# A second matrix product in two halves of the array that exchange their banks

## The chip, the cores and the metric

The kernel runs on one core of one Trainium2 chip. What is compared is the time on the device in microseconds of one execution. The engines are PE (TensorE, matrix products), DVE (VectorE), ACT (ScalarE), POOL (GpSimd) and SP (SyncE, which here issues transfers and waits).

## What is computed

A short convolution over the tokens of each of 8 sequences (7 taps, one softmax-normalised set of taps for each of 8 groups of 24 channels), and then a feed-forward part on each of the 31232 tokens:

```python
# B, S, D = 8, 3904, 192; H, K = 8, 7; d_ff = 1024
w = softmax(weight, axis=-1)                     # (H, K)
y[b, s, h, :] = sum_k w[h, k] * x_pad[b, s + k, h, :]     # 6 rows of zeros ahead of each sequence
a = y @ w1                                       # (31232, 1024)
b = y @ w2
h = a * b @ w3                                   # elementwise a*b, then (1024, 1024)
out = h @ w_out                                  # (31232, 192), float32
```

## The kernel before

Since nothing stands between the last two products, the kernel forms `W = w3 @ w_out` (1024 x 192, `W_sb`, eight tiles of 128 rows) once on the chip. For each token there are then two stages, here called the first and the second product: `a * b` (bf16, `abT`, 128 feature rows at a time, tokens along the free side), and `abT` times `W_sb`.

**Rounds.** The tokens lie in two streams of 15616 (`r` = 0 and 1, `NS = 2`). A round `R` takes 512 tokens of each stream (`CH`); there are 31 rounds, the last of 256. `abT` of a round is `[128, 8, 2, 512]`.

**First product** (`first_product`, L618 to L651). The depth is 192, cut into three pieces of 64 (`NP`, `Q`). Stream 0 has its channels on partitions 0 to 63 and stream 1 on 64 to 127, so matmuls use 64 rows of the array (64*128 in the profile) and come in pairs, one on each half, with 512 columns, into the two banks of a PSUM tile. For each of 8 feature tiles there are three pairs for `a` (`pa`) and three for `b` (`pb`). ACT casts `pa` to bf16 (`asb`, L640), DVE multiplies it with `pb` into `abT` (L643).

**Second product** (`second_product`, L653 to L677). For one round and stream: four groups of 128 tokens, eight feature tiles each, 32 matmuls with 128 rows and 192 columns (128*128 in the profile, L659), where the tile of `abT` is the loaded weight and `W_sb` streams. Two groups share a bank: group `g` lies in bank `g // 2`. ACT copies the two banks to `osb` (L664), SP stores `osb` (L673).

**PSUM.** All PSUM tiles are of one kind, `[128, 2, 512]` float32, two banks each (`banks`, L104). There are four, given out in turn.

**Phases.** The loop at L901 runs over 11 phases. In most of them it does the first product of three rounds (`rounds`) and then the second product of the same three rounds (`ends`), both streams of each. Phases are numbered `p` = 0 to 10 here, as in the code. In phases 0, 2 and 5 (`places`) part of the convolution is done on PE between the second products (`convolve`).

**The convolution of the other tokens.** For the phases in `SIDE` the convolution is a sum of scaled shifts, done on DVE (`side_sums`, six steps of about 1.3 us for a task, placed among the second products by `side_steps`) and on POOL (`pool_sums`). ACT does a first step of each (`side_first`, `pool_first`). Their inputs are brought in and transposed by DMA: `side_transpose` (L515) and `pool_transpose` (L568). Tokens convolved on PE are stored to DRAM and come back through `transposes` (L449, three or two transposes for a round).

**Order.** The schedule is by hand (`manual_schedule`): each engine's queue holds its instructions in the order in which the program issues them. All transposes and all result stores are on SP's queue. In the loop, after the first products of a phase: `turn(p)` issues the `transposes` that are due and whose place in the ring of rounds is free; then come the `pool_transpose` and `side_transpose` of the phase; then, for each round and stream, the second product with its copy and store and the side steps; at the end the `late` ones of `side_transpose` and another `turn(p)`.

Of the kernel before, what the change touches and what calls it, by code (L numbers as in the profile page):

```python
# [16 lines left out]
def kernel(  # L17
# [10 lines left out]
    nc = tc.nc  # L28

    B, S, D = x.shape  # L30
# [3 lines left out]
    JT = DFF // 128  # L34
    PAD = K - 1

    NS = 2
    TS = B * S // NS
    CH = 512
# [4 lines left out]
    Q = 64  # L44
# [59 lines left out]
    def banks(name):  # L104
        return psum.tile([128, NS, CH], FP32, tag="banks", name=name)
# [4 lines left out]
    def slot(shape, dtype, name):  # L110
        return stage.tile(shape, dtype, tag="slot", bufs=6, name=name)

    rows = dram.tile([TS, NP * NS * Q], BF16, name="rows")
# [15 lines left out]
    def group(r, e):  # L129
        return slice((2 * r + e) * C, (2 * r + e) * C + C)  # L130
# [57 lines left out]
    for r in range(NS):  # L188
        p = group(r, 0).start
# [110 lines left out]
    p = group(1, 0).start  # L300
# [3 lines left out]
    for k in range(2):  # L304
# [3 lines left out]
            start=(k == 0), stop=(k == 1))  # L308
# [134 lines left out]
    def transposes(R, first=0):  # L443
        t0, t1 = max(R * CH, first), min((R + 1) * CH, TS)
        a = ring_of[R] * CH % RING + t0 - R * CH
        for k in range(NP):
            if beside(phase_of(R), k):
                continue
            nc.sync.dma_start_transpose(  # L449
                out=xT[k][:, a:a + t1 - t0], in_=rows[t0:t1, k * 128:(k + 1) * 128])  # L450
# [98 lines left out]
    def pool_tiles():  # L549
        for t in (stage.tile([128, 3 * CH + HALO], BF16, tag="wo", bufs=1, name="acc"), pool_more):  # L550
            pool_acc.append(t[:, 0:2 * CH].bitcast(FP32))
            pool_raw.append(t[:, 2 * CH:3 * CH + HALO])

    def part_tile():
        t = work.tile([128, XN], BF16, tag="xb", bufs=5, name="side")
        o = 0
        for q, ks in PART.items():
            n = len(ks) * 2 * CH
            side_of[q] = t[:, o:o + n].rearrange("p (k t) -> p k t", k=len(ks))
            o += n  # L560
# [5 lines left out]
    def pool_transpose(lane, p, k, half):  # L566
        _, _, t0, _ = pool_half(p, k, half)
        nc.sync.dma_start_transpose(out=pool_raw[lane], in_=rows_c[t0 - HALO:t0 + CH, k, :])  # L568

    def pool_first(lane, p, k, half):  # L570
        nc.scalar.activation(
            out=pool_acc[lane], in_=pool_raw[lane][:, HALO - 1:HALO - 1 + CH],
            func=ACT.Copy, scale=wC[:, k, K - 2:K - 1])
# [39 lines left out]
    abT_of, asb_of = {}, {}  # L613

    def width(R):
        return min(CH, TS - R * CH)
# [33 lines left out]
            if between and f0 in between:  # L650
                between[f0]()  # L651

    def second_product(R, r, later=None):  # L653
        ab = abT_of[R]
        ng = width(R) // 128
        ops = banks("ops")
        for g in range(ng):
            for jt in range(JT):
                nc.tensor.matmul(  # L659
                    ops[:, g // 2, (g % 2) * D:(g % 2) * D + D],  # L660
                    ab[:, jt, r, g * 128:(g + 1) * 128], W_sb[:, jt, :],
                    start=(jt == 0), stop=(jt == JT - 1))
        osb = slot([128, ng, D], FP32, "osb")
        nc.scalar.copy(out=osb.rearrange("p (a g) d -> p a (g d)", g=2),  # L664
                       in_=ops[:, 0:ng // 2, 0:2 * D])
        n = ng if R < NR - 4 else ng // 2
        for g in range(0, ng, n):
            t0 = r * TS + R * CH + g * 128
            send = (nc.scalar if g and (R, r) == (NR - 1, NS - 2) else nc.sync).dma_start
            args = dict(out=out[t0:t0 + n * 128, :].rearrange("(g p) d -> p g d", p=128),  # L670
                        in_=osb[:, g:g + n, :])
            if later is None:
                send(**args)  # L673
            else:
                later.append(lambda send=send, args=args: send(**args))
        if r == 1:
            del abT_of[R]  # L677
# [15 lines left out]
    W_sb = const.tile([128, JT, D], BF16)  # L693
# [69 lines left out]
    phases = [((), trios[0])] + [(t, t) for t in trios[1:-1]] + \  # L763
        [(trios[-1], trios[-1][:1]), ((NR - 1,), trios[-1][1:] + (NR - 1,))]

    def stage_of(R):
        return R // TRIO

    places = {0: (1, 2, 3, 4), 2: (0, 1, 2, 3), 5: (0, 1, 3)}
# [4 lines left out]
    starts, chain, begun, room, p = {}, {}, set(), 0, -1  # L774
    for i, cost, f in steps:
        while room < cost:
            p += 1
            room = rooms[p]
            at, ends = 0, {}
            starts.setdefault(p, [])  # L780
        if i not in begun:
            begun.add(i)
            starts[p].append(i)
            n = max(p == 0, int(at) // 2 - 1, -(-ends.get(i - 2, 0) // 2))
# [9 lines left out]
    def side_steps(p, n, state):  # L794
        items = chain.get(p, [])
        for v, (i, at, f) in enumerate(items):
            if at is not None and at <= n and v not in state:
                state.add(v)
                f()
        for v, (i, at, f) in enumerate(items):  # L800
            if at is None and v not in state:
                state.add(v)
                f()
            elif v not in state:
                break
# [46 lines left out]
    for p, b, part, n in ((1, 5, 0, 0), (1, 5, 1, 4), (3, 6, 0, 0), (4, 6, 1, 0)):  # L852
        todo = x_jobs(b, part)
        n = n or len(todo)
        jobs[p] += todo[:n]
        jobs[p + 1] += todo[n:]
    pool_from = {p - 1: v for p, v in POOL_AT.items()}
# [11 lines left out]
    sent, rest, results = [LAG + 3], [], []  # L869
# [20 lines left out]
    def turn(p):  # L890
        while due and stage_of(due[0]) <= p + 2 and \
                stage_of(conv_rounds[ring_of[due[0]] - RING // CH]) <= p:
            transposes(due.pop(0))

    def clear():
        for b in list(zero_rows):
            for xb, p0, w in zero_rows.pop(b):
                nc.gpsimd.memset(xb[p0:p0 + PAD, w, :], 0.0)

    pace = const.tile([1, 2], BF16)  # L900
    for p, (rounds, ends) in enumerate(phases):  # L901
        todo = jobs.pop(p, [])

        last = len(points) - 1
        lanes = pool_sum.pop(p, ())
        counts = [0] * 7 if len(lanes) > 1 else [0] * 3 + [2] * 4 if p == 1 else [2] * 2 + [1] * 5
        at = [[todo.pop(0) for _ in range(min(n, len(todo)))] for n in counts + [len(todo)]]
        if p in places:
            at[last - 1].insert(0, clear)
        elif len(lanes) > 1:  # L910
            at[last].insert(0, clear)
        for fs in lanes:
            for v, f in enumerate(fs):
                at[v if len(lanes) == 1 else 0].append(f)
        if p == 3:
            part_tile()

        def issue(R, ft, fs):
            def run():
                P(out=pace, in_=abT_of[R][0:1, ft, 1, 0:2] if ft else asb_of[0][0:1, 1, 0:2])  # L920
                for f in fs:
                    f()
            return run

        for j, R in enumerate(rounds):
            first_product(R, {ft: issue(R, ft, at[v])
                              for v, (a, ft) in enumerate(((0, 0),) + points[1:] if
                                                          len(lanes) > 1 else points)
                              if a == j and at[v]})
        assert not todo  # L930
        if len(lanes) < 2:
            clear()
        if p == 0:
            pool_tiles()
        turn(p)
        raws = starts.get(p + 1, ())
        late = [i for i in raws if p == 0 or len(lanes) > 1 or i >= 5 and chain[p][0][0] <= i - 5]
        if p > 1:
            for lane, t in enumerate(pool_from.get(p, ())):
                pool_transpose(lane, *t)  # L940
        for i in raws:
            if i not in late:
                side_transpose(i)
        if p == 1:
            pool_transpose(0, *pool_from[p][0])
        state = set()
        side_steps(p, 0, state)
        for n, (R, r) in enumerate((R, r) for R in ends for r in range(NS)):
            if (R, r) == (NR - 1, NS - 1):
                last_product(R, r)  # L950
            else:
                second_product(R, r, results if p == 0 else None)
            if n == 4 and len(pool_from.get(p, ())) > 1:
                for lane, t in enumerate(pool_from[p]):
                    pool_first(lane, *t)
            if n in places.get(p, ()):
                convolve(p)
            side_steps(p, n + 1, state)
        assert len(state) == len(chain.get(p, ()))
        while results:  # L960
            results.pop(0)()
        for b, js in rest:
            store(b, js=js)
        rest.clear()
        for i in late:
            side_transpose(i)
        turn(p)
# [31 lines left out]
```

## Time and profile before

| | us |
|---|---|
| median of 3 runs | 510.65 (510.35 to 510.77) |
| the profiled execution | 510.84 |
| its span | 509.1 |

| engine | busy us | share | instructions |
|---|---|---|---|
| PE matmuls | 504.4 | 99% | 5732 |
| PE weight loads (PEld) | 335.9 | 66% | 5732 |
| DVE | 446.2 | 88% | 402 |
| ACT | 349.6 | 69% | 390 |
| POOL | 255.9 | 50% | 340 |

All stretches of the span show PE's granted clock at nine tenths or more of full speed. In the rows of the time line the columns are the start in us, the time in us from the first start to the last end of the merged instructions, engine, line, operation, what is written and read, and the number of instructions; a bracket holds idle time before them and what ended it. SPq is the queue of SP. In the rows of the chain of waits the columns are start, duration, engine, tile and line. In the rows of a stretch (`197.30:213.30`) they are its length, the busy time of PE, PEld, DVE, ACT and POOL with the number of instructions, the granted clock of PE, and the share and rate of the DMA engines.

### The profile page before, as it was taken

What the parts mean: (1) busy time and instruction counts of PE and PEld (TensorE: products, weight loads), DVE (VectorE), ACT (ScalarE), POOL (GpSimd) and SP (SyncE); (2) the same over time, 40 slices, a digit from 0 to 9 for tenths busy, and PEclk for the clock granted to TensorE, in tenths of its full rate; (3) what the DMA queues carried; (4) which work ended last, traced back from release to release, by engine and by line L of the source; (5) the groups of instructions that cost most, each with busy time, mean ns of one, the idle gap of its engine ahead of it and who ended that gap; (6) DMA issues with size and microseconds to landing.
All of it is one profiled execution on the core that took longest, in us unless ns stands there. A gap on an engine that the chain in (4) does not pass through costs nothing.

```text
span 509.1 us, 13680 instructions
## 1 busy us (share of the span) xinstructions
PE 504.4 (99%) x5732; PEld 335.9 (66%) x5732; DVE 446.2 (88%) x402; ACT 349.6 (69%) x390; POOL 255.9 (50%) x340
## 2 busy tenths in 40 slices
PE   8999999999999999999999999999999999999997
PEld 4546864595569557845874596569457855965697
DVE  7898769999999799999999998999999999999930
ACT  6786667746779776577567878763876577457752
POOL 9975201332890799499879945992371056000000
PEclk9999999999999999999999999999999999999999
DMA  9999978999969769980998097629302400230025
GB/s 136 160 170 162 166 150 182 149 156 182 175 41 181 136 150 108 227 110 13 100 232 103 12 167 145 117 29 202 83 1 76 155 2 1 93 96 1 1 65 156
DMA packets 161113, 58.46 MB, mean 115 GB/s; under 512 B 116895, under 2 KB 161051, under 8 KB 161051
## 3 DMA queue, kind: packets, MB, share of 16 engines
q1 hardware_dynamic: 86107, 40.12, 37.7%
q0 software_dynamic: 74784, 17.37, 37.3%
q8 instruction: 45, 0.74, 0.6%
q14 instruction: 17, 0.14, 0.1%
q10 hardware_dynamic: 160, 0.10, 0.1%
HBM read 35.02 MB, written 34.85 MB: 137 GB/s over the span
## 4 chain that ended last, share of the span: by engine, by line
PE 99%; ACT 0%; DVE 0%; issue 0%
PE ops L659 32%; PE pa L633 31%; PE pb L633 31%; PE cps L345 1%; PE wps L731 1%; PE warm L246 1%; PE tps L420 0%; PE ops L684 0%; DVE abT L643 0%; PE tps L435 0%; PE cps L375 0%; ACT asb L640 0%; ACT convo L355 0%; PE bps L305 0%; PE warm L258 0%
## 5 line engine op out<-in xcount | busy, mean ns | idle before, releaser
L643 DVE TENSOR_TENSOR abT<-asb,pb 128x1024 bf16<-128x1024 bf16 x240 | 292.7, 1221 | 29.4 <-ACT asb L640 13.4
L640 ACT CAST asb<-pa 128x1024 bf16<-128x1024 f32 x244 | 247.0, 1012 | 64.0 <-PE pa L633 63.8
L633 PEld LDWEIGHTS <-wn 64*128 64x128 bf16 x1488 | 138.5, 94 | 82.1 <-issue 1.6
L633 PEld LDWEIGHTS <-ws 64*128 64x128 bf16 x1488 | 130.1, 94 | 70.8 <-issue 0.9
L659 PE MATMUL ops<-W_sb,abT 128*128 128x192 bf16 x1936 | 163.5, 246 | 0.0
L659 PEld LDWEIGHTS <-abT 128*128 128x128 bf16 x1936 | 158.6, 98 | 6.3 <-issue 6.3
L664 ACT COPY osb<-ops 128x768 f32<-128x768 f32 (+1 forms) x61 | 48.5, 796 | 81.8 <-PE ops L659 80.0
L633 PE MATMUL pb<-xT,wn 64*128 64x512 bf16 x376 | 103.7, 376 | 0.0
L633 PE MATMUL pa<-xT,ws 64*128 64x512 bf16 x376 | 103.5, 376 | 0.0
L633 PE MATMUL pa<-xT,wn 64*128 64x512 bf16 x376 | 103.0, 376 | 0.1
L633 PE MATMUL pb<-xT,ws 64*128 64x512 bf16 x376 | 102.2, 376 | 0.0
L633 PE MATMUL pb<-side,wn 64*128 64x512 bf16 (+1 forms) x368 | 100.4, 369 | 0.0
L633 PE MATMUL pa<-side,ws 64*128 64x512 bf16 (+1 forms) x368 | 99.4, 369 | 0.0
L633 PE MATMUL pa<-side,wn 64*128 64x512 bf16 (+1 forms) x368 | 99.4, 369 | 0.0
L633 PE MATMUL pb<-side,ws 64*128 64x512 bf16 (+1 forms) x368 | 98.1, 369 | 0.0
L538 DVE SCALAR_TENSOR_TENSOR acc<-raw,wC,acc 128x1024 f32<-128x1024 bf16 (+2 forms) x70 | 84.5, 1208 | 2.1
L596 POOL TENSOR_TENSOR acc<-acc,tmp 128x512 f32<-128x512 f32 (+6 forms) x60 | 70.4, 1177 | 4.3
L584 POOL TENSOR_TENSOR tmp<-acc,wC 128x512 f32<-128x512 bf16 x66 | 68.5, 1038 | 3.5
L920 POOL COPY pace<-abT 1x2 bf16<-1x2 bf16 x28 | 4.9, 174 | 110.0 <-DVE abT L643 110.0
L506 POOL DMA_DIRECT2D rows_c<-in_x_dram x58 | 40.7, 710 | 5.7 <-issue 2.9
L165 POOL DMA_DIRECT2D xb<-in_x_dram x50 | 31.9, 647 | 11.2 <-DMA xb<-in_x_dram 5.0
L538 DVE SCALAR_TENSOR_TENSOR acc<-side,wC,acc 128x1024 f32<-128x1024 bf16 (+1 forms) x20 | 24.4, 1218 | 3.9 <-ACT acc L520 3.4
(83 smaller groups left out, 190.6 us busy)
## 6 DMA issues: line engine op xcount, KB each, us to landing
out_dram<-osb SPq DMA_DIRECT2D x54, 384.0 KB
xb<-in_x_dram POOLq DMA_DIRECT2D x16, 240.0 KB, 7.5
out_dram<-osb SPq DMA_DIRECT2D x12, 192.0 KB
rows_c<-in_x_dram POOLq DMA_DIRECT2D x14, 130.0 KB, 6.9
rows_c<-in_x_dram POOLq DMA_DIRECT2D x14, 128.0 KB, 4.6
xb<-in_x_dram POOLq DMA_DIRECT2D x6, 228.0 KB, 7.9
w3b<-in_moe_w_dram POOLq DMA_DIRECT2D x4, 256.0 KB, 5.0
w3b<-in_moe_w_dram POOLq DMA_DIRECT2D x8, 128.0 KB, 4.3
```

The source lines that it names most:

```text
L165: nc.gpsimd.dma_start(out=tiles[js[0]][0][group(r, e), s:s + w, :], in_=bass.AP(tensor=x.tensor, offset=(r * TS + t - PAD) * D, ap=[[D, C] ...
L246: nc.tensor.matmul(t[:, j % 2, 0:wd].rearrange("p (a c) -> p a c", c=128), zeros, zeros.unsqueeze(1).to_broadcast([128, wd // 128, 128]), ...
L345: nc.tensor.matmul(o.rearrange("p (w g) -> p w g", g=wd)[:, :, c - c0:c1 - c0], Aband[group(r, e), h, :], xb[group(r, e), s:s + m, c:c1], ...
L506: nc.gpsimd.dma_start(out=rows_c[lo:t1, k, r * Q:r * Q + Q], in_=x_rows[r * TS + lo:r * TS + t1, k * Q:k * Q + Q])
L538: nc.vector.scalar_tensor_tensor(out=side_of[p][:, k, o:o + t1 - t0] if last else a, in0=raw[:, HALO + lo - t0 - d:HALO + hi - t0 - d], sc ...
L584: nc.gpsimd.tensor_tensor(out=acc if d == 1 else tmp, in0=pool_raw[lane][:, HALO - d:HALO - d + CH], in1=wC[:, k, K - 1 - d:K - d].to_broa ...
L596: nc.gpsimd.tensor_tensor(out=a, in0=a, in1=tmp[:, lo - t0:hi - t0], op=ALU.add)
L633: nc.tensor.matmul(p[:, r, f * N:f * N + N], w_of(i, k, r)[rs, ft * 128:(ft + 1) * 128], operand(R, k, rs), start=(k == 0), stop=(k == NP ...
L640: nc.scalar.copy(out=asb[:, :, 0:per * N], in_=pa[:, :, 0:per * N])
L643: nc.vector.tensor_tensor(out=ab[:, f0, :, 0:N], in0=asb[:, :, 0:N], in1=pb[:, :, 0:N], op=ALU.mult)
L659: nc.tensor.matmul(ops[:, g // 2, (g % 2) * D:(g % 2) * D + D], ab[:, jt, r, g * 128:(g + 1) * 128], W_sb[:, jt, :], start=(jt == 0), stop ...
L664: nc.scalar.copy(out=osb.rearrange("p (a g) d -> p a (g d)", g=2), in_=ops[:, 0:ng // 2, 0:2 * D])
```

## The change

In phases 3, 4, 6, 7 and 8 (`halves`) the second product of a round is issued for both streams at once by a new function, `half_rows`, with 64 rows of the array in each matmul. Each half of the rows holds half of the depth of each feature tile, so each output needs both halves. In the first turn (`turn = 0`) half 0 works on the two token groups of bank 0 and half 1 on those of bank 1; in the second turn they change banks and add the other half of the depth. The order is: first turn of stream 0, of stream 1, second turn of stream 0, of stream 1. Behind the first turn of each stream an instruction is put in SP's queue that only waits for it (`relay`), and the first matmul of the second turn waits for the relay. Two PSUM tiles are held at once.

The matmuls of the first of the three rounds are issued ahead of `turn(p)` and the transposes of the phase; those of the second and third ahead of their round's copies. With them the relays take their places in SP's queue: those of the first round ahead of the phase's transposes, those of the second behind these and behind the first round's stores. `side_steps` runs once more at the start of a round, and `pool_first` ahead of the copy that it followed.

```diff
+    def half_rows(R):
+        ab = abT_of[R]
+        assert width(R) == CH
+        opss = [banks("ops") for _ in range(NS)]
+        sync = mybir.DependencyInfo(mybir.DependencyClass.Sync, mybir.DependencyReason.DATA)
+        why = "the banks pass to the other half of the rows"
+        handed = {}
+        for turn in range(2):
+            for r in range(NS):
+                for g in range(2):
+                    for jt in range(JT):
+                        for h in range(2):
+                            a = h ^ turn
+                            rs, q = slice(Q * h, Q * h + Q), 2 * a + g
+                            mm = nc.tensor.matmul(
+                                opss[r][:, a, g * D:g * D + D],
+                                ab[rs, jt, r, q * 128:(q + 1) * 128], W_sb[rs, jt, :],
+                                start=(turn == 0 and g == 0 and jt == 0),
+                                stop=(turn == 1 and g == 1 and jt == JT - 1))
+                            if turn == 1 and (g, jt) == (0, 0):
+                                tc.add_manual_dep(mm.ins, handed[r], sync, reason=why)
+                if turn == 0:
+                    relay = nc.sync.nop()
+                    tc.add_manual_dep(relay.ins, mm.ins.name, sync, reason=why)
+                    handed[r] = relay.ins.name
+        return opss
...
-    def second_product(R, r, later=None):
+    def second_product(R, r, later=None, ops=None):
...
+        if ops is None:
             ...  # the matmuls as before
...
         if p == 0:
             pool_tiles()
+        halves = 2 < p < len(phases) - 2 and p not in places
+        opss = half_rows(ends[0]) if halves else (None, None)
         turn(p)
...
         for n, (R, r) in enumerate((R, r) for R in ends for r in range(NS)):
+            own_first = n == 4 and len(pool_from.get(p, ())) > 1
+            if halves and r == 0:
+                if n:
+                    opss = half_rows(R)
+                side_steps(p, n + 1, state)
+            if halves and own_first:
+                for lane, t in enumerate(pool_from[p]):
+                    pool_first(lane, *t)
             if (R, r) == (NR - 1, NS - 1):
                 last_product(R, r)
             else:
-                second_product(R, r, results if p == 0 else None)
-            if n == 4 and len(pool_from.get(p, ())) > 1:
+                second_product(R, r, results if p == 0 else None, opss[r])
+            if own_first and not halves:
```

More of the change, by code (lines that the diff above doesn't have):

```diff
@@ L651, in first_product @@
                 between[f0]()
-    def second_product(R, r, later=None):
+    def half_rows(R):
[25 more added lines that the diff above has]
+    def second_product(R, r, later=None, ops=None):
         ab = abT_of[R]
         ng = width(R) // 128
[L656 to L662, printed above, removed]
+        if ops is None:
+            ops = banks("ops")
+            for g in range(ng):
+                for jt in range(JT):
+                    nc.tensor.matmul(
+                        ops[:, g // 2, (g % 2) * D:(g % 2) * D + D],
+                        ab[:, jt, r, g * 128:(g + 1) * 128], W_sb[:, jt, :],
+                        start=(jt == 0), stop=(jt == JT - 1))
         osb = slot([128, ng, D], FP32, "osb")
```

## The prediction

> **What bounds the kernel now.** I read the page's busy shares and its chain first, then the chain of waits around one second product, then the time line of single matmuls, and last the time line of SP's queue.
>
> ```profile
> PE 504.4 (99%) x5732; PEld 335.9 (66%) x5732; DVE 446.2 (88%) x402; ACT 349.6 (69%) x390; POOL 255.9 (50%) x340
> PE 99%; ACT 0%; DVE 0%; issue 0%
> ```
>
> TensorE carries 99% of the chain that ended last. A microsecond taken from PE is therefore a microsecond of the run, and so is one that PE waits. Around the second product of phase 3 the chain reads (start, duration):
>
> ```profile
> 196.78 0.65 PE pb L633 x6
> 197.42 15.95 PE ops L659 x192
> 213.37 0.75 PE pa L633 x6
> ```
>
> Six half-array matmuls of the first product take 0.65 us, so each pair takes 0.216 us. The 192 full-array matmuls of three rounds take 15.95 us. Single matmuls at both ends of that stretch:
>
> ```profile
> 197.04 0.38 PE L633 MATMUL pb<-side,ws 64*128 64x512 bf16 x1
> 197.05 0.38 PE L633 MATMUL pb<-side,wn 64*128 64x512 bf16 x1
> 197.35 0.42 PE L659 MATMUL ops<-W_sb,abT 128*128 128x192 bf16 x3
> ...
> 199.76 13.61 PE L659 MATMUL ops<-W_sb,abT 128*128 128x192 bf16 x163
> ...
> 213.30 0.39 PE L633 MATMUL pa<-side,wn 64*128 64x512 bf16 x1
> 213.30 0.60 PE L633 MATMUL pa<-side,ws 64*128 64x512 bf16 x2
> 213.53 0.38 PE L633 MATMUL pa<-side,wn 64*128 64x512 bf16 x1
> ```
>
> A 64*128 matmul on one half starts 0.01 us or less behind its partner on the other: the halves run together. Inside the second product a matmul starts every (13.61 - 0.25)/162 = 0.0825 us (one lasts 0.25), and the last starts at 199.76 + 13.36 = 213.12.
>
> **The mode switches that go.** Into the second product PE takes 197.35 - 197.05 = 0.30 us where a pair takes 0.216: 0.09 lost. Out of it, 213.30 - 213.12 = 0.18 instead of 0.0825, 0.10 lost, and the first pair lasts 213.53 - 213.30 = 0.23, 0.01 more. That is 0.20 us a phase; in five phases both sides of the product are then half-array, so 5 x 0.20 = **-1.0 us**. The row of the switch agrees with the Trainium skill, "TensorEngine Tiling (Array Packing)", Key Properties, by which a change of tiling mode drains the array.
>
> **The same products as pairs.** Each second product becomes 64 half-array matmuls instead of 32 full ones, 32 pairs; five phases x 6 products x 32 = 960 pairs. No row has a 64x192 pair. The nearest are the 64x256 pairs of the last round, and the loads:
>
> ```profile
> 491.54 0.27 PE L633 MATMUL pa<-side,wn 64*128 64x256 bf16 x1
> 491.54 0.27 PE L633 MATMUL pa<-side,ws 64*128 64x256 bf16 x1
> 491.65 0.27 PE L633 MATMUL pb<-side,wn 64*128 64x256 bf16 x1
> 491.76 0.27 PE L633 MATMUL pb<-side,wn 64*128 64x256 bf16 x1
> ...
> L659 PEld LDWEIGHTS <-abT 128*128 128x128 bf16 x1936 | 158.6, 98 | 6.3 <-issue 6.3
> L633 PEld LDWEIGHTS <-wn 64*128 64x128 bf16 x1488 | 138.5, 94 | 82.1 <-issue 1.6
> ```
>
> A pair with two loads fits in 0.11 us at 256 columns and 0.216 at 512, in proportion to the columns; 192/256 x 0.11 gives 0.0825, today's pace. It cannot be much less (columns) and by these rows not over 0.11 (if the two loads were what takes the time there): **0 to +26 us** over 960 pairs. I take 0, because the 512 and 256 rows scale with columns and a 98 ns load already hides under a matmul every 82.5 ns.
>
> One rule speaks against that. The Trainium skill, "TensorE: Matmul & The Clock Gate", Part 3, says that a weight load overlaps running matmuls only when its row group differs; a later load for the same half would then lie open. By that rule some 0.094 us would come to each pair, +90 us. The L659 rows disagree: those loads use all the rows that the running matmul uses, and still one matmul starts every 0.0825 us.
>
> **The new wait.** Half h starts in bank h and changes to the other. The first load of the second turn waits for a relay: an instruction that only waits, in SP's queue, behind the last matmul of the first turn. Two relays a round, 30 in all. A relay passes only when SP reaches it, and SP takes its queue in order. The queue of the changed program stands so: relays of round 1; then the transposes that the phase issues (`turn`, `pool_transpose`, `side_transpose`), which stood ahead of the second product and now stand behind those relays; the two result stores of round 1; relays of round 2; stores; relays of round 3. What SP has to do between the relays of rounds 1 and 2 differs by phase, and SP is not quick at it:
>
> ```profile
> 180.46 16.55 SPq L449 DMA_TRANSPOSE xT<-rows  x12
> 197.18 2.45 SPq L568 DMA_TRANSPOSE acc<-rows_c  x2
> 201.03 13.57 SPq L673 DMA_DIRECT2D out_dram<-osb  x6
> ...
> 244.26 1.12 SPq L568 DMA_TRANSPOSE acc<-rows_c  x1
> ...
> 319.96 11.19 SPq L449 DMA_TRANSPOSE xT<-rows  x8
> 331.31 1.14 SPq L568 DMA_TRANSPOSE acc<-rows_c  x1
> 343.82 0.37 SPq L673 DMA_DIRECT2D out_dram<-osb  x1
> ...
> 385.13 1.44 SPq L568 DMA_TRANSPOSE acc<-rows_c  x1
> 386.74 5.01 SPq L515 DMA_TRANSPOSE raw<-rows_c  x4
> 391.85 7.39 SPq L673 DMA_DIRECT2D out_dram<-osb  x4
> ```
>
> Twelve transposes take SP from 180.46 to 197.18, 1.39 us each; a store 0.37, some 0.42 with the gap behind it. For the hand-over I use the copies:
>
> ```profile
> 200.21 0.80 ACT L664 COPY osb<-ops 128x768 f32<-128x768 f32 x1 [1.33 <-PE ops L659]
> 202.84 0.80 ACT L664 COPY osb<-ops 128x768 f32<-128x768 f32 x1 [1.84 <-PE ops L659]
> ```
>
> The first product's last matmul starts at 197.35 + 31 x 0.0825 = 199.91 and its reader at 200.21: 0.30 us. Let t0 be the start of the halves. Round 1's second relay follows 32 pairs and passes at t0 + 31 x 0.0825 + 0.30 = t0 + 2.86. Round 2 needs its first relay when 64 pairs of round 1 and 32 of its own are through: 96 x 0.0825 = t0 + 7.92. The stores of round 1 can go at t0 + 4.2 + 0.8 = 5.0 and 5.5 + 0.8 = 6.3, so without transposes the relay passes near t0 + 6.9, when its matmuls are through. Slack: 1.0 us. With transposes, the halves would start 0.16 before these rows of the chain, as in phase 3 (197.42 against 197.05 + 0.216 = 197.26):
>
> ```profile
> 244.56 15.95 PE ops L659 x192
> ...
> 340.21 15.95 PE ops L659 x192
> ...
> 387.35 15.95 PE ops L659 x192
> ```
>
> - Phase 3: t0 = 197.26. Of the twelve xT transposes six stand behind the relays, and both of `pool_transpose`. 197.26 + 2.86 + 6 x 1.39 + 2 x 1.25 (197.18 to their end, 199.68) + 2 x 0.42 + 0.1 for the hand-over = 211.9; needed at 205.2. **+6.7 us** of PE idle. At 1.26 to 1.55 us a transpose it is 6.0 to 8.0.
> - Phase 7: five transposes, from 385.13 to the store at 391.85, 6.7 us, and stores that take some 0.5 each there. t0 = 387.19: 387.19 + 2.86 + 6.7 + 1.0 + 0.1 = 397.8, needed at 395.1. **+2.7 us** (2.3 to 3.3).
> - Phase 6: two xT at 11.35/8 = 1.42 and one of 1.2: t0 + 2.86 + 4.0 + 0.84 + 0.1 = t0 + 7.8 against 7.92. 0, up to 0.5.
> - Phase 4: two of 1.2: t0 + 5.3, then the stores at 6.3: 0. SP's wait for POOL there ended at 244.26, before t0 = 244.40. Phase 8 has none: 0.
>
> Round 3's relays stand behind stores alone, slack 1.0 again. The transposes themselves lose no reader: the delayed ones feed later phases. The matching first relays come ahead of them. Nothing takes the lost time back, since PE has no other idle time.
>
> **The clock after a stall.** PE has no gap of 6.7 us today. The rows nearest to it are those ahead of its first and behind its last matmul:
>
> ```profile
> L684 PE MATMUL ops<-W_sb,abT x16: 246/246/246, 504.3 to 505.5; 128*128 128x192 bf16 x16
> 508.10:509.10 1.00, 0.00 (x0) 0.00 (x0) 0.00 (x0) 0.00 (x0) 0.00 (x0) 0.53 0.00 0
> 1.07 2.74 PE L246 MATMUL warm<-zeros 128*128 128x512 bf16 x6 [1.07 <-DVE zeros L187]
> 6.01 0.58 PE L258 MATMUL warm<-Aband,zeros 128*128 128x256 bf16 x2
> ```
>
> The last matmul ends at 505.7, and by 508.1 the granted clock (0.53) is near half. At the start 128x512 matmuls last so long that six take 2.74 us, and at 6.01 two of 256 columns still take 0.58 together, where one lasted 0.27 above and starts came 0.11 apart: half speed from 1.07 to 6.2. So a drop costs at most about 5.2/2 = 2.6 us. The start has gaps that lengthen it; I take 1.5 for phase 3's gap, and 0.5 for phase 7's, which is hardly longer than the 2.4 us after which the clock fell: **+2.0 us**, 0 to 5. The Trainium skill, "TensorE: Matmul & The Clock Gate", Part 1, has the window in which activity is judged at about 3.4 us; by a strict reading phase 7 would keep its clock and the sum would be 0.5 less.
>
> Smaller: 30 loads carry a wait. 28 find it met; if each such load lost its cover, 30 x 0.09 = 2.7 us; I take 0, since the awaited first matmul of a product costs nothing beyond the switch today. ACT's copies keep their number; both copies of a round end by t0 + 6.3 as now. Sum: 6.7 + 2.7 + 2.0 - 1.0 = +10.4. The profiled execution took 510.84 us, its span 509.1; the median of the runs is 510.65, 0.2 below it. 510.65 + 10.4 = **521.0 us**.
>
> **Rivals.**
> - *The switch alone counts* (relays pass in time: SP would have to be through with its transposes before the relay is due). 510.65 - 1.0 = 509.65, faster. It decides where no more than 7.92 - 2.86 - 0.84 - 0.1 = 4.1 us of transposes, three of them, stand between the relays of rounds 1 and 2; against it, eight at 1.39 us in phase 3. Chance 0.06.
> - *Loads or issue pace the pairs.* At 0.09 to 0.11 us a pair, +7 to +26, less the part of SP's delay that slower pairs cover (round 2 needs its relay later): 525 to 540. For it: no 64x192 pair is on record. Chance 0.10, the part with the Trainium skill's rule (+90 us, about 600) 0.01 of that.
> - *SP does its transposes at a third of the time* when nothing else is on its queue, 0.5 us each: phase 3 would stop for under 1 us, about what the switches give, 510.65. Against it: the twelve of today follow each other without a wait. Chance 0.02.
> - Forecast, 518 to 526 with its bounds: 0.82.
>
> DVE is no rival (busy us of PE, PEld and DVE in phase 3's product):
>
> ```profile
> 197.30:213.30 16.00, 16.00 (x194) 15.79 (x193) 15.61 (x13) 7.85 (x10) 11.01 (x18) 1.00 1.50 186
> ```
>
> It fills 15.6 of 16.0 us, but a stalled PE only gives it time.
>
> The range **517 to 527** takes the forecast's bounds and the lower end of slow pairs. A difference of 0.2% (1 us) is about what can be told from none. Faster by that 0.06, same 0.02, slower 0.92.
>
> **What would show it.** In phase 3 the matmuls of round 2 stop at about t0 + 7.9 for 6 to 8 us, with SP's queue full of transposes; a shorter stop in phase 7, none in 4 and 8; pairs every 0.0825 us; 0.216 us across both borders; a granted clock below 1 behind phase 3's stop. Wrong if phase 3 shows no stop, or if pairs start 0.09 us apart or more.

## The result: slower by 3.5%, and the profile after

The changed kernel takes 528.4 us (median of 6 runs, 527.3 to 529.7) against 510.65 for the kernel before, ratio 1.0348 (95% interval 1.0329 to 1.0366). The profiled executions took 528.68 and 510.84 us: 17.8 us more, where the prediction had 10.4. In the changed kernel the new matmuls are L667, the relay is L675 and the stores are L701. From the page of the profile after: busy shares, granted clock in 40 slices, the chain, and the group of the new matmuls with what ended the idle time before them:

```profile
PE 506.0 (96%) x6692; PEld 338.2 (64%) x6692; DVE 446.5 (85%) x402; ACT 349.2 (66%) x390; POOL 256.4 (49%) x340
PEclk9999999999999999699999999999999999999999
PE 85%; POOL 6%; SPq 2%; DVE 2%; DMA 1%; issue 1%; ACT 1%; POOLq 0%
L667 PE MATMUL ops<-W_sb,abT 64*128 64x192 bf16 x1920 | 83.0, 246 | 16.4 <-SPq L675 14.6
```

PE is still the longest engine, but its busy share fell from 99% to 96%; it waited 14.6 us for L675, which is the relay in SP's queue. The chain of waits through phase 3 shows what SP was doing (start, duration):

```profile
197.38 7.93 PE ops L667 x192
...
205.40 1.21 SPq L449
...
206.71 1.33 SPq L449
...
208.13 2.05 SPq L449
...
210.35 1.49 SPq L568
...
212.00 2.07 SPq L568
...
214.18 0.53 SPq L701
...
214.80 1.23 SPq L701
...
216.08 0.02 SPq L675
...
216.14 8.90 PE ops L667 x157
```

PE runs 7.93 us of pairs, as many as fit before round 2 needs its relay. Then the chain is SP alone, transpose by transpose, and two stores, until the relay at 216.08. PE resumes at 216.14. The other stops, in the time line of PE (idle time and what ended it in brackets), in phases 4, 6 and 7:

```profile
272.05 0.75 PE L667 MATMUL ops<-W_sb,abT 64*128 64x192 bf16 x14 [1.74 <-issue]
...
363.52 0.67 PE L667 MATMUL ops<-W_sb,abT 64*128 64x192 bf16 x12 [0.72 <-SPq L675]
...
413.69 0.67 PE L667 MATMUL ops<-W_sb,abT 64*128 64x192 bf16 x12 [3.08 <-SPq L675]
```

Two ended on a relay. That of phase 4 ended on nothing that the profile shows (`issue`); it falls behind the 310th matmul of the product, 54 matmuls into a turn of round 3, where neither a relay nor a new bank is due. The clock behind phase 3's stop, in stretches (length, busy us of PE, PEld, DVE, ACT, POOL, granted clock, DMA share, GB/s):

```profile
205.30:216.10 10.80, 0.00 (x1) 0.00 (x0) 9.12 (x8) 0.00 (x0) 4.13 (x7) 0.74 1.96 156
216.10:220.60 4.50, 4.46 (x58) 4.18 (x60) 0.00 (x0) 0.80 (x1) 0.00 (x0) 0.50 1.29 263
220.60:226.20 5.60, 5.60 (x139) 5.59 (x135) 0.00 (x0) 2.83 (x4) 0.00 (x0) 0.99 0.54 174
```

For 4.5 us PE ran at half speed: 28 pairs started 0.16 us apart instead of 0.0825, so 2.2 us were lost. Phase 8, which has no transposes on SP, shows what the change does by itself. Its chain, and the borders of phase 3 in the time line:

```profile
452.28 0.65 PE pb L633 x6
452.93 15.84 PE ops L667 x384
468.77 0.65 PE pa L633 x6
```

```profile
197.01 0.38 PE L633 MATMUL pb<-side,wn 64*128 64x512 bf16 x1
197.22 0.33 PE L667 MATMUL ops<-W_sb,abT 64*128 64x192 bf16 x4
...
225.70 0.74 PE L667 MATMUL ops<-W_sb,abT 64*128 64x192 bf16 x14
226.28 0.38 PE L633 MATMUL pa<-side,wn 64*128 64x512 bf16 x1
226.28 0.59 PE L633 MATMUL pa<-side,ws 64*128 64x512 bf16 x2
226.50 0.38 PE L633 MATMUL pa<-side,wn 64*128 64x512 bf16 x1
```

384 half-array matmuls, 192 pairs, take 15.84 us: 0.0825 each. Into the product PE takes 0.21 instead of 0.30, and the first pair behind it lasts 0.22 and not 0.23. From the last first-product pair to the first pair of the next phase, phase 8's product took 16.04 us where it took 16.25 before.

### The profile page after: what moved, and what is told of

Same layout as the page of the kernel before. It is cut to its first block, busy times and chain, and to the rows that moved or that the text cites. A ratio compares the mean times of both kernels' runs of the same rounds, so it can differ in the third digit from the quotient of the medians.

```text
span 527.0 us, 15630 instructions
## 1 busy us (share of the span) xinstructions
PE 506.0 (96%) x6692; PEld 338.2 (64%) x6692; DVE 446.5 (85%) x402; ACT 349.2 (66%) x390; POOL 256.4 (49%) x340
## 4 chain that ended last, share of the span: by engine, by line
PE 85%; POOL 6%; SPq 2%; DVE 2%; DMA 1%; issue 1%; ACT 1%; POOLq 0%
PE pa L633 27%; PE pb L633 27%; PE ops L687 16%; PE ops L667 13%; POOL acc L596 2%; POOL tmp L584 2%; DVE acc L538 1%; PE cps L345 1%; PE wps L759 1%; SPq L568 1%; SPq L449 1%; DMA xb<-in_x_dram 1%; DMA rows_c<-in_x_dram 1%; SPq L701 1%; ACT asb L640 1%
## 5 line engine op out<-in xcount | busy, mean ns | idle before, releaser
L667 PE MATMUL ops<-W_sb,abT 64*128 64x192 bf16 x1920 | 83.0, 246 | 16.4 <-SPq L675 14.6
L667 PEld LDWEIGHTS <-abT 64*128 64x128 bf16 x1920 | 81.1, 96 | 18.7 <-SPq L675 15.3
L687 PE MATMUL ops<-W_sb,abT 128*128 128x192 bf16 x976 | 83.5, 246 | 0.0
L687 PEld LDWEIGHTS <-abT 128*128 128x128 bf16 x976 | 79.6, 98 | 4.1 <-issue 4.1
```

Source lines behind the costliest of these rows:

```text
L667: mm = nc.tensor.matmul(opss[r][:, a, g * D:g * D + D], ab[rs, jt, r, q * 128:(q + 1) * 128], W_sb[rs, jt, :], start=(turn == 0 and g == 0 ...
L687: nc.tensor.matmul(ops[:, g // 2, (g % 2) * D:(g % 2) * D + D], ab[:, jt, r, g * 128:(g + 1) * 128], W_sb[:, jt, :], start=(jt == 0), stop ...
```

## The experiments

Theory 1: the pairs and the borders do what they should; PE waits because the relays of round 2 stand in SP's queue behind transposes and stores. Rival: products in halves, or handing over the banks, cost the time. Where an experiment changes which phases have their products in halves, `halves` is the only line changed for that.

**Relays in another queue** (`e1_act`).

```diff
-                    relay = nc.sync.nop()
+                    relay = nc.scalar.nop()
...
-        opss = half_rows(ends[0]) if halves else (None, None)
         turn(p)
...
         side_steps(p, 0, state)
+        opss = half_rows(ends[0]) if halves else (None, None)
```

> Relays stand in ACT's queue instead of SP's; the matmuls of the first round are issued behind the first side steps, so that ACT's first step is not held. Theory 1 (PE waits because the relays of round 2 stand behind transposes and stores on SP): the stops of phases 3, 6 and 7 (11.0, 0.9, 3.2 us) and the low clock behind the first (2.2 us) go, the switches saved (1.0) stay: 509.7 us; 1.9 more (511.6) if the stop in phase 4, which ended on no relay, stays. Rival (the products in pairs or the hand-over of the banks themselves cost the time): 520 us or more.

Measured: 509.95 us, ratio to the kernel before 0.9986 (0.9978 to 0.9995). The rival falls: with the same matmuls and a hand-over of the same kind through another queue, 18 us are gone. Phases 4, 6, 7 and 8 take 16.04 to 16.05 us between first products, 0.2 less than before. Phase 3 kept one short stop. Its chain:

```profile
197.27 14.11 PE ops L667 x342
211.38 0.19 issue
211.57 1.91 PE ops L667 x42
```

The matmul behind that stop starts 0.44 us behind the one ahead of it, and no relay is near.

**Relays on SP, behind the transposes** (`e2_behind`).

```diff
-        opss = half_rows(ends[0]) if halves else (None, None)
         turn(p)
...
             pool_transpose(0, *pool_from[p][0])
+        opss = half_rows(ends[0]) if halves else (None, None)
         state = set()
```

> Relays stay in SP's queue; the matmuls and relays of the first round are issued behind the phase's transposes. Theory 1: nothing but stores stands between the relays of rounds 1 and 2, so the stops of phases 3 and 6 go. In phase 7 the relays of round 1 now stand behind five transposes of 6.7 us that cannot start before 2.1 us ahead of the product, so PE stops there some 2.0 us in round 1 instead of 3.2 in round 2: 510.65 - 1.0 + 2.0 = 511.7 us, 513.6 if the stop of phase 4 stays. Rival (pairs or banks themselves): 520 or more.

Measured: 514.8 us, 1.0086 (1.0071 to 1.0101). The stop of round 2 is gone in phases 3, 6 and 7, and the relay of round 1 stops phase 7, as theory 1 had it, but for longer. The time line of SP and PE in phase 7, and the stretch of its product:

```profile
385.39 1.12 SPq L568 DMA_TRANSPOSE acc<-rows_c  x1
386.70 6.04 SPq L515 DMA_TRANSPOSE raw<-rows_c  x4
...
392.85 1.43 PE L667 MATMUL ops<-W_sb,abT 64*128 64x192 bf16 x24 [2.60 <-SPq L675]
```

```profile
387.30:407.70 20.40, 17.80 (x388) 17.25 (x386) 16.99 (x17) 7.20 (x9) 0.00 (x0) 0.92 0.36 100
```

SP was through at 392.7. The matmuls ahead of the stop and behind it started 2.85 us apart, so 2.8 us were lost instead of 2.0. The clock fell too (0.92 over the stretch). Phase 7 took 20.5 us instead of 16.25; phase 3 had one stop of 0.84 us without a relay.

**Phase 3 alone** (`e3_only3`, `halves = p == 3`).

> Only phase 3 has the product in halves. Theory 1: its share alone, 11.0 us of stop and 2.2 of low clock less 0.2: +13.0, 523.7 us. Rival (a cost of each product in halves, the same in all five): a fifth of +17.9, 514.2 us.

Measured: 522.1 us, 1.0219 (1.0203 to 1.0234): nearer to theory 1's 523.7 than to the rival's 514.2. Phase 3 took 28.35 us between first products (29.27 in the changed kernel), with a gap of 9.5 us (11.1) from one matmul to the next, at the same place. The other phases took 16.25 as before. So the stop's length varies: in the same phase SP's eight transposes took 12.4 us here and its two stores 1.7, against 13.9 and 1.9 in the changed kernel. The shorter stop met more of the low clock, which cost 2.9 us here.

**Phase 4 alone** (`e4_only4`, `halves = p == 4`).

> Only phase 4 has the product in halves. If the 1.9 us stop in its round 3, which ended on no relay in the profile, belongs to the products in halves there (twice the instructions in the same time): +1.7, 512.4 us, with the stop in the profile again. If it came from transfers that phase 3's long stop had moved: 510.45 us and no stop.

Measured: 510.84 us, 1.0005 (0.9996 to 1.0014), between the two. The profile has a stop again, of 0.57 us from the matmul at 259.85 to the next, and on no relay. So it is not a result of phase 3's stop, but its length varies: 2.0 us in the changed kernel.

**POOL's loads beside SP's transposes** (`e6_held3`). In phase 3 POOL issues sixteen loads about when SP reaches the delayed transposes. Here they wait for a result copy of round 2.

```diff
-    abT_of, asb_of = {}, {}
+    abT_of, asb_of, osb_of = {}, {}, {}
...
+        osb_of[0] = osb
...
+        held = []
+        if p == 3:
+            held, at[last] = at[last], []
...
-        halves = 2 < p < len(phases) - 2 and p not in places
+        halves = p == 3
...
+            if n == 4 and held:
+                P(out=pace, in_=osb_of[0][0:1, 0, 0:2])
+                for f in held:
+                    f()
```

> Only phase 3 in halves, relays on SP; POOL's sixteen loads of that phase wait for the copies of the second round instead of running beside SP's transposes. Theory (the transposes took 1.1 to 2.6 us instead of 1.2 because POOL's transfers ran beside them): eight transposes at 1.2 to 1.3 us and two stores at 0.4 to 0.5, PE stops for 6 to 7 us instead of 9.4 to 11.0, phase 3's product takes some 24.5 to 25.5 us between first products instead of 28.4; 519 to 520 us if nothing later waits for the held loads. Rival (transposes behind a product in halves are that slow by themselves): stop of 9 us or more, 522 us.

Measured: SP's time line and PE's resumption:

```profile
200.26 8.70 SPq L449 DMA_TRANSPOSE xT<-rows  x6
209.13 2.44 SPq L568 DMA_TRANSPOSE acc<-rows_c  x2
211.67 1.07 SPq L702 DMA_DIRECT2D out_dram<-osb  x2
...
212.85 0.98 PE L667 MATMUL ops<-W_sb,abT 64*128 64x192 bf16 x10 [7.47 <-SPq L675]
```

Eight transposes took 11.3 us from 200.26, seven of them 1.14 to 1.21 us each and the first 2.2, where the changed kernel's took 13.9 from 200.19, 1.1 to 2.6 each. The gap at the relay is 7.7 us, above the 6 to 7 expected and well under 9.4 to 11.1; phase 3 took 25.95. In the changed kernel the DMA engines' share in that time was 1.96 (row above). Here it was 0.40:

```profile
200.20:212.80 12.60, 5.18 (x126) 4.95 (x121) 12.28 (x11) 2.65 (x3) 0.00 (x0) 0.92 0.40 86
```

and in the changed kernel, while the first six transposes ran at 1.2 us but for one, 0.66:

```profile
181.30:189.80 8.50, 8.50 (x82) 4.33 (x80) 8.00 (x7) 6.80 (x7) 7.95 (x8) 1.00 0.66 169
```

The kernel that differs from this run in the held loads alone is `e3_only3`. Its stretch:

```profile
200.00:214.30 14.30, 5.11 (x124) 4.88 (x120) 13.94 (x12) 2.65 (x3) 8.43 (x14) 0.85 1.73 161
```

Against its 12.4 and 1.7 us, the transposes took 11.3 and the stores 1.1, and the gap was 7.7 us instead of 9.5. That is 1.8 us less without the loads, in one profile each. But between `e3_only3` and the changed kernel, which both have the loads, the gaps differ by 1.6 us, and with the loads held the stop is still 0.9 us over the 6.7 of the prediction, half of it in the transposes, of which the first took 2.2 us. All 924 transposes on SP's queue in the eleven profiles point the same way: of the 571 with POOL's queue busy for less than 2% of the engines' time, 16% took over 1.4 us (mean 1.32); of the other 353, 41% did (mean 1.52). So slow transposes are more frequent beside POOL's loads, but not peculiar to them, and what makes the others slow is not shown. The run as a whole was 526.0 us, 1.0295 (1.0273 to 1.0318): the held loads came too late for the next phase, where PE stopped for 4.1 us and went on slowly; the 519 to 520 expected on condition that nothing waits for them did not come.

**The short stops of phases 3 and 4.** A product in halves has twice the instructions of PE in the same time. The trace shows instructions being fetched by DMA (queue q8, 16 KB at a time). Theory: beside POOL's transfers a fetch comes too late. `e7_held4` has phase 4 alone in halves and holds POOL's loads of phase 4 with the edit above (`p == 4` in both places).

> Only phase 4 in halves, relays on SP; POOL's loads of that phase wait for the copies of the second round. Theory (the short stops of phases 3 and 4 that end on no relay are late fetches of instructions, held up by POOL's transfers): no stop in phase 4 before the held loads start, product between first products 16.05 us. Rival (late by themselves at twice the rate of instructions): a stop of 0.4 to 2 us as before.

Measured: no such stop in phase 4. One gap of 0.27 us stands at 251.93, where round 2 takes its relay from SP; it cost the 0.2 that the borders gave (16.25 us, not 16.05). 517.6 us in all, 1.0128 (1.0111 to 1.0144), all of it behind the held loads, in the next phase.

`e8_free134` has the relays in ACT's queue and halves in phases 1, 3 and 4 (`halves = p in (1, 3, 4)`); `e9_held34` the relays in ACT's queue, halves in phases 3 and 4, and the loads of both held.

> Relays in ACT's queue, products in halves in phases 1, 3 and 4 alone, the phases whose products run beside POOL's transfers. Theory (late fetches of instructions beside POOL's transfers): stops of 0.3 to 2 us that end on no relay in at least one, more likely two of the three, so that their 0.6 us of saved switches are lost: ratio 0.9995 to 1.002. Rival (those stops came with relays on SP or with the long stop): none over 0.2 us, 0.6 us saved, ratio 0.9988.

> Relays in ACT's queue, products in halves in phases 3 and 4, POOL's loads of these phases wait for the copies of the second round, some 11.5 us into the product. Theory (late fetches beside POOL's transfers): no stop over 0.2 us in the first 11.5 us of either product, where earlier profiles have them at 13 to 15 us, and one behind that point is possible. The run as a whole is slower, some 520 us, because later work waits for the held loads. Rival (late fetches at twice the rate of instructions in any case): a stop of 0.4 us or more ahead of the loads.

Measured: `e8_free134` took 512.2 us, 1.0031 (1.0015 to 1.0047), slower than before by 0.3% and worse than expected. Its stops in phases 1 and 4, in the time line:

```profile
114.40 0.59 PE L667 MATMUL ops<-W_sb,abT 64*128 64x192 bf16 x10 [1.56 <-issue]
...
261.52 0.51 PE L667 MATMUL ops<-W_sb,abT 64*128 64x192 bf16 x8 [0.17 <-issue]
```

The DMA queues between 101 and 113 us, in phase 1 ahead of its stop (packets, MB, share of 16 engines):

```profile
q0 software_dynamic: 3166, 1.18, 97.3%
q1 hardware_dynamic: 2904, 0.70, 73.2%
q8 instruction: 2, 0.03, 1.0%
```

`e9_held34` (one run, 526.2 us, slowed by the held loads as the two before) had no gap over 0.1 us in either product, before or behind the loads: 16.05 and 16.04 us. Queue q0, that of POOL's loads, is empty until they start. Over the profiles, the fetch ahead of a stop began 6.6 to 10.2 us behind the one before it, and PE went on 1.3 to 1.6 us after it had landed; in phase 8, without stops, fetches follow each other at 4.6 to 6.3 us. The interval alone does not decide: 7.2 to 7.9 us passed without a stop in phase 3 of `e8_free134`, in phase 4 of `e1_act` and `e2_behind`, and in phase 6 of `e2_behind` and `e5_best`. Over all profiles, of the nine products in halves in phases 1, 3 and 4 that ran beside POOL's loads and had no relay to wait for, six had such a stop; of the three with the loads held, none; of those in phases 6 to 9, none. So the stops go with POOL's transfers and come at twice the rate of instructions, but not every time. That a late fetch is the means is read from times that fit; no run moved a fetch by itself, and the cause stays open.

**Halves only where POOL is idle or light** (`e5_best`): the relays in ACT's queue as above, and

```diff
-        halves = 2 < p < len(phases) - 2 and p not in places
+        halves = 5 < p < len(phases) - 1
```

> Relays in ACT's queue as in the run with ACT's relays, products in halves in phases 6 to 9 alone, where the share of the DMA engines is half or less of that in phases 3 and 4. Theory: 0.2 us saved in each of four phases and no stop: 0.8 us under the kernel before, ratio 0.9984, no stop over 0.3 us in the profile. Rival (the short stops come with products in halves anywhere): stops of 0.4 to 2 us in some of these phases, ratio 0.999 or more.

Measured: 509.78 us, ratio 0.9981 (0.9972 to 0.9990), without a stop. Phases 6, 7 and 8 took 16.04 to 16.05 us, phase 9 5.48 (5.70 before). Phase 6 is not as light as was expected: the DMA share over its product is 1.08, against 1.50 and 1.46 in phases 3 and 4 of the kernel before. Phase 7's chain:

```profile
386.83 0.65 PE pb L633 x6
387.48 15.84 PE ops L667 x384
403.32 0.65 PE pa L633 x6
```

It beats both kernels by the little that the borders hold.

## Why the prediction was right and wrong

The mechanism and its places were right: PE waits for relays of round 2 in phases 3 and 7, because SP has transposes ahead of them. The direction was right, the size not: the sum of the stops was too small, and 528.4 lies outside 517 to 527.

| term | predicted us | measured in the profile after |
|---|---|---|
| borders, five phases | -1.0 | -1.0 (0.2 each, phase 8 and `e1_act`) |
| pace of pairs | 0 | 0 (15.84 / 192 = 0.0825) |
| stop, phase 3 | +6.7 (6.0 to 8.0) | +11.0 (9.4 in `e3_only3`) |
| stop, phase 7 | +2.7 (2.3 to 3.3) | +3.2 |
| stop, phase 6 | 0 (to 0.5) | +0.9 |
| stop, phase 4 | 0 | +1.9 |
| clock | +2.0 (0 to 5) | +2.2 |
| sum | +10.4 | +18.2; the whole execution +17.8, with 0.3 less behind PE's last matmul |

- **The step that failed most** is the price of SP's work in phase 3. Eight transposes and two stores were given 10.8 + 0.84 us; they took 13.9 + 1.9 in the changed kernel and 12.4 + 1.7 in `e3_only3`. The price per transpose was read at 180 to 197 us, where the DMA share was 0.57, and applied at 200 to 214, beside POOL's loads, where it was 1.73 to 1.96. `e6_held3` took the loads away and gave 11.3 + 1.1. By that the loads are 1.8 us of the 2.7 by which `e3_only3` passed the prediction; the further 1.6 of the changed kernel are a difference between two profiles with the same loads, whose cause stays open. The row for it stood in the prediction: phase 3's product has a DMA share of 1.50. (One reading there is off by 0.05 us: the two transposes from 197.18 end at 199.63, not 199.68.)
- **Phase 4** was given nothing because its relay comes in time. It does; the stop is another one. The prediction bounded the doubled instructions only by the pace of pairs, where steady rows are, and gave nothing to what else can hold them up. `e8_free134` and `e9_held34` showed that such stops come beside POOL's transfers; what they wait for is not shown.
- **Phases 6 and 7** are the same error as phase 3, but small: the first transpose of phase 6 took 1.95 us instead of 1.42, the last of phase 7 took 1.51 instead of the 1.24 of the kernel before, and stores took 0.5.
- **The clock**: the loss behind phase 3 was 2.2 us, not 1.5, and 2.9 in `e3_only3`, over the 2.6 that the prediction took as the most. Behind phase 7's 3.2 us it did not fall (0.5 had been put there), and in `e2_behind` it fell behind 2.8 us. The traces say why. Within a profile the granted clock changes only at marks that lie whole multiples of 3.41 us apart, and what counts is how much of one stretch between two marks PE was idle. The stretches in phase 7, the first two of the changed kernel, the last two of `e2_behind`:

```profile
408.47:411.89 3.42, 2.15 (x53) 1.92 (x48) 3.35 (x3) 0.97 (x2) 0.00 (x0) 1.00 0.62 101
411.89:415.30 3.41, 1.61 (x40) 1.61 (x42) 3.27 (x6) 1.00 (x2) 0.00 (x0) 1.00 0.62 181
390.19:393.60 3.41, 0.81 (x20) 0.75 (x20) 3.30 (x4) 0.00 (x0) 0.00 (x0) 1.00 0.32 59
393.60:397.01 3.41, 3.41 (x49) 3.20 (x46) 3.34 (x3) 0.80 (x1) 0.00 (x0) 0.50 0.09 27
```

The longer gap was split by a mark, 1.27 us idle and 1.80; the shorter one lay almost whole in one stretch, 2.60 us idle, and the next stretch ran at half clock. Over the eleven profiles, from 20 us on, a full clock fell behind every stretch with 2.27 us of idle or more and behind none with 1.92 or less. The Trainium skill has the clock judged by a window of about 3.4 us ("TensorE: Matmul & The Clock Gate", Part 1) and lets it fall after one idle window. The length agrees with these marks; but the window need not be idle throughout, since 2.60 us of 3.41 were enough here.
- **The rivals.** "The switch alone counts" is what the relays in ACT's queue give: 0.7 us under before, where the rival had 1.0; phase 3's short stop cost 0.4. Loads do not pace the pairs: 64x192 pairs start every 0.0825 us. So the rule of the Trainium skill ("TensorE: Matmul & The Clock Gate", Part 3) that a load overlaps only other row groups' matmuls does not hold here.
- **What was taken as free** was free: the waits that are met cost nothing (phase 8 has six and takes 15.84 us; 27 were met, not 28, as phase 6's was late too), and copies and side steps did not delay PE.

## What to carry to other kernels

A wait that one engine hands on through another's queue costs what stands in that queue ahead of it: list those instructions for each place, and choose a queue whose work is finished by then. Price them in the stretch where they will run, with the transfers that run there, not where they run today. A reordering that saves 0.2 us at a border can lose more than that if it doubles the instructions of an engine beside heavy transfers: phase 1 of `e8_free134` lost 1.5 us.

## What was not expected of the hardware

- A transpose issued by SP mostly takes 1.2 us. Over 1.4 us took 41% of those beside POOL's transfers and 16% of the others, the slowest 3.9 and 2.8 us.
- PE, at twice its usual number of instructions, stopped for 0.4 to 2.0 us without waiting for any engine, in phases with POOL's transfers only, and there in six products of nine.
- Behind a gap of 11 us PE ran at a granted clock of 0.50 for 4.5 us. A gap of 2.8 us lowered the clock and one of 3.2 did not, because marks 3.41 us apart split the longer one.
